# Fused attention, soft MoE and squared-ReLU FFN on one core: w_out slots 2 to 7 converted as pairs, the later m sums and the column sum as two fp32r products behind ReLU, two evictions ahead of a conversion

## The chip, the core and the metric

The kernel runs on one core of a Trainium2 chip. The metric is device time in microseconds (us) of the whole program. Three timed runs of the kernel before gave a median of 480.83 us (479.24 to 481.24). A fourth execution was recorded by the profiler.

## The reference

Three layers follow each other. All tensors are fp32.

```python
# 1. chunked attention: 4 batches, 8 heads, 768 positions, head size 64; chunks of 32 see 16 left, 8 right, 8 memory slots
a = softmax(q_c @ k_full.T / 8);  attn = a @ v_full          # -> x: (3072, 512)
# 2. soft MoE: 8 experts with 4 slots each
logits = x @ phi                                             # (3072, 32)
slot_input = softmax(logits, axis=0).T @ x                   # (32, 512)
slot_out = relu(slot_input[e] @ w1[e]) @ w2[e]               # (32, 512), F = 1024
y = softmax(logits, axis=1) @ slot_out                       # (3072, 512)
# 3. squared-ReLU FFN: d_ff = 2048
out = (s * relu(y @ w_in)**2 + b) @ w_out                    # (3072, 512)
```

## The kernel before

**Stages.** From the start to about 167 us the kernel runs attention, the routing softmaxes and the experts; the weights of the experts (w1, w2: 33.5 MB) stream from HBM through one queue on SP. From about 168 us to the end it runs the FFN, and there the change has its effect.

**The FFN's items.** y is never formed. Instead m = slot_out @ w_in (32 x 2048) is kept in `mpack`, and h = c @ m, with the routing weights c in `cpack`. The work is cut into 128 items, each one a block of 384 rows (b) with a slice of 128 of the 2048 hidden columns (f). Items 0 to 15 take blocks 0 and 1 in turn with f = 0 to 7, items 16 to 47 blocks 2 and 3 in turn with all 16 f, then come blocks 4 to 7 with 16 items each, and last the second halves of blocks 0 and 1. One item is

- on TensorE (PE): one product for h (`emit_h`, L825, 384 columns, fp32r), six products of 512 columns with the high half of w_out (`emit_o`, L877: three row tiles, once with the high and once with the low half of g) and three with its low half (`emit_o2`, L889);
- on ScalarE (ACT): ReLU (L831), square (L835), and the cast to the fp32r high half ghi (L839);
- on VectorE (DVE): the low half glo = g - ghi (`emit_g`, L842).

Iteration n of the main loop (it starts at n = 4) emits h of item n, ReLU, square and ghi of n, glo of n - 1, the high products of item n - 3 and the low products of n - 4. Each engine works through its instructions in the order in which the code emits them; a wait on one holds all behind it on that engine.

**Exact products.** TensorE's fp32r takes an operand rounded. So a factor is split in a rounded high half and the rest, and three products are added up. A plain fp32 product (L806, L812, L852) stands in the trace as two slower matmuls.

**Conversions.** w_in and w_out arrive as pairs of 16-bit halves. A slice of 512 columns is rebuilt by one ACT step (`cv_act`, L579) and by DVE steps: shift (L589), sign (L591), mask (L593), low part (L600). For w_out, ACT then casts the high half `whi` (L798) and DVE makes `wlo` in two steps (L791, L793). The table `cq` says at which iteration k which slice is converted: w_out slices f = 0 to 7 at k = 0, 2, ..., 14 (slice f is first used by item 2f), eight slices of w_in at k = 16 to 30, w_out slices 8 to 15 at k = 32 to 46. `stage_a`, `stage_d` and `stage_w` emit the steps of key k at iterations k - 1, k and k + 1. A w_out "slot" i holds the raw slices 2i and 2i + 1; three areas (NRG) take the raw slots in turn, and `load_w` at the loop's end loads the next one once the area's last use is over.

**The m sums.** `M_AT = (4, 26, 34)`: at these iterations `emit_m` forms a quarter of m in four row groups (L806), ACT copies it out of PSUM (`mps`, L808), one iteration later `emit_m2` adds the four groups up with a product by the 0/1 matrix `stks_all` (L812), and `m_split` writes `mpack` (ACT L817, DVE L818). The h products, the m sums and the column sum share two PSUM banks (tag "s"); a bank is taken again once the engines that read it are done. The sums are emitted ahead of the iteration's ReLU.

**Ends of blocks.** After the last f of a block the three accumulators are moved out of PSUM (L896 on DVE for tiles 0 and 2, L894 on ACT for tile 1) before the next block with the same banks may start. For blocks 0 and 1 this is at n = 18 and n = 19.

**Column sum.** At n = 64 `colsum` (L852) multiplies a matrix of ones with the sum of w_out to get b times the column sums, the `bias` of the later evictions.

## Time and profile before

| | |
|---|---|
| median of three runs | 480.83 us (479.24 to 481.24) |
| profiled execution | 479.52 us, of it 477.7 us from the first to the last instruction |
| PE busy | 456.7 us (96%) |
| DVE busy | 310.1 us (65%) |
| ACT busy | 308.7 us (65%) |
| granted TensorE clock | 1.00 of full speed |
| DMA | about 400 GB/s until 167 us, then under 170 GB/s |

Matmuls are pipelined: one is shown busy until its result has landed, and the next begins before that. So what a matmul costs is the time from its start to the next one's start, and a gap in a PE timeline is told by such starts.

### The profile page before, as it was taken

Reading aid. Unit: us, or ns where it says so; the run is one execution under the profiler, and the core shown is the slowest. Engines: PE = TensorE matmul, PEld = TensorE weight load, DVE = VectorE, ACT = ScalarE, POOL = GpSimd, SP = SyncE. Lnnn points to the kernel's source line nnn. Section 1 sums busy time; section 2 is a strip of 40 time slices with the busy share of each in tenths; the row PEclk is TensorE's granted clock in tenths of the full one; section 3 lists DMA queues with packets and bytes.
Section 4 is the critical chain, followed back from the end, with each engine's and each line's share of the span. In section 5 each row is a group of like instructions: output and inputs, shape, how many; then the busy total and the mean of one; then the engine's idle time right before and its main releaser. Section 6 shows DMA issues by size and latency. Waiting matters only on the chain.

```text
span 477.7 us, 10206 instructions
## 1 busy us (share of the span) xinstructions
PE 456.7 (96%) x3960; PEld 342.3 (72%) x3960; DVE 310.1 (65%) x685; ACT 308.7 (65%) x635; POOL 84.4 (18%) x154
## 2 busy tenths in 40 slices
PE   7899998999999999999898999999999999999996
PEld 5666666665555467868585888888888888888885
DVE  6778887885485889997484999975524224223232
ACT  4566666675144388888576897666666666666660
POOL 6666665650000000000000000007700000000000
PEclk9999999999999999999999999999999999999999
DMA  8999999999999934234222000003101001001011
GB/s 304 385 406 405 406 409 398 397 381 396 401 420 392 414 128 151 89 99 166 88 89 88 1 1 0 1 0 146 55 0 67 0 1 67 0 1 66 1 67 66
DMA packets 20576, 83.04 MB, mean 174 GB/s; under 512 B 2736, under 2 KB 2864, under 8 KB 14640
## 3 DMA queue, kind: packets, MB, share of 16 engines
q1 hardware_dynamic: 20528, 82.39, 44.6%
q8 instruction: 31, 0.51, 0.4%
q14 instruction: 17, 0.14, 0.1%
HBM read 76.09 MB, written 6.29 MB: 172 GB/s over the span
## 4 chain that ended last, share of the span: by engine, by line
PE 69%; DVE 13%; DMA 8%; ACT 4%; issue 3%; SPq 2%; POOL 1%; DVEq 0%; POOLq 0%; ACTq 0%
PE g L877 11%; PE lp L877 5%; PE pt L877 5%; PE x L877 5%; PE g L889 5%; PE xt L877 5%; PE s L825 4%; DMA seg<-in_w_dram 4%; PE s L630 3%; PE x L325 3%; DMA vals<-in_vm_dram 3%; PE lp L889 3%; PE pt L889 3%; PE xt L889 3%; PE x L889 3%
## 5 line engine op out<-in xcount | busy, mean ns | idle before, releaser
L842 DVE TENSOR_TENSOR glo<-r,ghi 128x384 fp32r<-128x384 f32 x128 | 76.3, 601 | 81.6 <-ACT ghi L839 81.4
L831 ACT ACTIVATE r<-s 128x384 f32<-128x384 f32 x128 | 62.8, 491 | 52.8 <-PE s L825 52.4
L835 ACT ACTIVATE r<-r 128x384 f32<-128x384 f32 x128 | 67.4, 527 | 6.2 <-DVE glo L842 2.0
L839 ACT CAST ghi<-r 128x384 fp32r<-128x384 f32 x128 | 65.7, 513 | 3.4
L825 PE MATMUL s<-cpack,mpack 128*128 128x384 f32 x128 | 44.2, 348 | 3.7 <-ACT r L831 2.1
L301 ACT ACTIVATE seg<-seg 128x384 f32<-128x384 f32 x32 | 28.8, 900 | 19.2 <-DVE seg L312 15.1
L889 PE MATMUL g<-wlo,ghi 128*128 128x512 f32 x128 | 40.2, 394 | 0.0
L877 PE MATMUL g<-whi,ghi 128*128 128x512 f32 x126 | 39.7, 394 | 0.2 <-DVE mpack L818 0.2
L877 PE MATMUL g<-whi,glo 128*128 128x512 f32 x126 | 39.3, 393 | 0.0
L864 POOL TENSOR_TENSOR keys<-keys,bias 128x512 f32<-128x512 f32 x6 | 8.4, 1426 | 168.7 <-DVE bias L853 168.7
L263 POOL TENSOR_SCALAR keys<-keys 64x416 f32<-64x416 f32 x63 | 33.7, 536 | 12.7 <-DMA keys<-in_kq_dram 7.5
L285 PE MATMUL s<-keys 128*32 128x128 f32 x768 | 30.3, 291 | 4.4 <-POOL keys L267 3.4
L825 PEld LDWEIGHTS s<-cpack,mpack 128*128 128x128 f32 x128 | 23.9, 188 | 13.0 <-ACT r L831 4.4
L325 PE MATMUL x<-vals,seg 128*32 128x128 f32 x744 | 28.0, 275 | 2.8 <-DMA vals<-in_vm_dram 2.0
L325 PEld LDWEIGHTS x<-vals,seg 128*32 128x32 f32 x744 | 20.3, 109 | 13.2 <-DVE seg L309 6.4
L889 PEld LDWEIGHTS g<-wlo,ghi 128*128 128x128 f32 x128 | 24.0, 188 | 5.3
L877 PEld LDWEIGHTS g<-whi,glo 128*128 128x128 f32 x126 | 23.7, 188 | 5.3
L285 PEld LDWEIGHTS s<-keys 128*32 128x32 f32 x768 | 19.5, 113 | 10.4 <-POOL keys L267 6.0
L319 ACT COPY seg<-pt 128x384 f32<-128x384 f32 x32 | 15.3, 478 | 17.9 <-PE pt L317 16.9
L877 PEld LDWEIGHTS g<-whi,ghi 128*128 128x128 f32 x126 | 23.7, 188 | 4.3 <-DVE mpack L818 0.7
L877 PE MATMUL lp<-whi,ghi 128*128 128x512 f32 x63 | 25.5, 404 | 0.9 <-DVE vals L896 0.9
L877 PE MATMUL pt<-whi,ghi 128*128 128x512 f32 x64 | 25.6, 400 | 0.0
(255 smaller groups left out, 991.1 us busy)
## 6 DMA issues: line engine op xcount, KB each, us to landing
seg<-in_w_dram SPq DMA_DIRECT2D x27, 1024.0 KB, 8.5
keys<-in_kq_dram SPq DMA_DIRECT2D x32, 396.0 KB, 7.4
vals<-in_vm_dram SPq DMA_DIRECT2D x64, 192.0 KB, 6.5
keys<-in_w_in_dram SPq DMA_DIRECT2D x5, 1024.0 KB, 5.1
keys<-in_w_out_dram SPq DMA_DIRECT2D x5, 1024.0 KB, 4.9
out_dram<-os SPq DMA_DIRECT2D x18, 256.0 KB, 2.1
vals<-in_w_in_dram SPq DMA_DIRECT2D x3, 1024.0 KB, 5.6
vals<-in_w_out_dram SPq DMA_DIRECT2D x3, 1024.0 KB, 4.9
```

The source lines that it names most:

```text
L263: (nc.vector if h and u == 0 else nc.gpsimd).tensor_scalar(out=stream(kz[rows, h], 0, CH), in0=k[rows, UT * h:UT * h + (NCU + 1) * CH].rea ...
L285: nc.tensor.matmul(out=o, lhsT=qt[:, 32 * c:32 * c + 32], rhs=kz[:, :, at:at + WIN], start=True, stop=not (first or last))
L301: nc.scalar.activation(out=p_r[u], in_=sm_r[u].rearrange("p t h (a r) -> p t r (h a)", a=2), func=AF.Exp, scale=scale)
L319: nc.scalar.copy(out=pts_r[u], in_=pt)
L325: nc.tensor.matmul(out=xp[32 * r:32 * r + 32, t], lhsT=pts_r[u][:, 32 * c:32 * c + 32], rhs=vbuf[u // 2 % 2][:, u % 2, :, 64 * c:64 * c + ...
L825: nc.tensor.matmul(out=hq, lhsT=mpack[:, 128 * f:128 * f + 128], rhs=cpack[:, b * UT:(b + 1) * UT], start=True, stop=True)
L831: nc.scalar.activation(out=r_g[n % 2], in_=h_t.pop(n), func=AF.Relu)
L835: nc.scalar.activation(out=r2_g[n % 2], in_=r_g[n % 2], func=AF.Square)
L839: nc.scalar.copy(out=ghi_g[n % (LA + 2)], in_=r2_g[n % 2])
L842: nc.vector.tensor_tensor(out=glo_g[n % (LA + 2)], in0=r2_g[n % 2], in1=ghi_g[n % (LA + 2)].bitcast(F32), op=ALU.subtract)
L877: nc.tensor.matmul(out=o_t[r_][t], lhsT=gt[:, 128 * t:128 * t + 128], rhs=w_hi[f], start=(f == r_[1] and gt is ghi), stop=False)
L889: nc.tensor.matmul(out=o, lhsT=ghi[:, 128 * t:128 * t + 128], rhs=w_lo[f], start=False, stop=(f == f1 - 1))
```

## The change

In the main loop:

- w_out slices 0 to 3 are converted as before. Slots 2 to 7 (slices 4 to 15) are converted as pairs of slices 1024 wide: `pair_a` (ACT) at iteration p0 - 1, shift and sign at p0, mask and low part and the cast `pair_hi` at p0 + 1, the two steps of `wlo` at p0 + 2 and p0 + 3, with p0 = 8, 11, 31, 34, 38 and 42 (table PS). All whi slices lie in one tile, all wlo slices in another. The conversion buffers and raw areas are placed elsewhere.
- `sums(n)` stands behind ReLU, square and ghi for n > 7. The second and third m sum and the column sum no longer use a plain fp32 product: `halves` makes a rounded copy on ACT (`mph`) and the rest on DVE (`mpl`), and `sum_of` multiplies both in fp32r.
- The conversion of iteration 18 is emitted in iteration 19, behind the evictions of block 1 (`convert(n - 1)`), and the load that would follow it waits for that, too.
- The load of the second raw slot is issued one step later in the w2 loop. Two small ACT instructions (`stkr`, `onesr`) make the fp32r matrices of the sums; a POOL memset of ones is gone.

```diff
--- before.py
+++ after.py
@@ -173,16 +173,16 @@
         at_.update({key: (18 + i) * SLOT for i, key in enumerate(EARLY)})
         cq = {}
         for j in range(8):
+            cq[16 + 2 * j] = ("i", 2 + j // 4, j % 4)
+        for j in range(4):
             cq[2 * j] = ("o", j)
-            cq[16 + 2 * j] = ("i", 2 + j // 4, j % 4)
-            cq[32 + 2 * j] = ("o", 8 + j)
-        raw_of = {("i", fb, j): ("wi", 2 * fb + j // 2) for fb in range(1, NFB) for j in range(4)}
-        raw_of.update({("o", f): ("wo", f // 2) for f in range(NF)})
-        last_use = {}
-        for k, key in sorted(cq.items()):
-            if raw_of[key] not in last_use:
-                order.append(raw_of[key])
-            last_use[raw_of[key]] = k
+
+        PS = {2: 8, 3: 11, 4: 31, 5: 34, 6: 38, 7: 42}
+        last_use = {("wi", 4 + j // 2): 16 + 2 * j for j in range(8)}
+        last_use.update({("wo", i): n + 1 for i, n in PS.items()})
+        last_use.update({("wo", 0): 2, ("wo", 1): 6})
+        order += [("wo", i) for i in range(4)] + [("wi", i) for i in range(4, 8)] + [("wo", i) for i in range(4, 8)]
+        RAW = [17 * SLOT, 18 * SLOT, 14 * SLOT]
         srcs = {"w1": w1, "w2": w2, "wi": w_in, "wo": w_out}
 
         wt = {}
@@ -193,7 +193,7 @@
                 i = wnext[0]
                 if i < (len(order) if cap is None else cap):
                     src = srcs[order[i][0]][order[i][1]]
-                    p = at_[order[i]] if i < npre else (16 + (i - npre) % NRG) * SLOT
+                    p = at_[order[i]] if i < npre else RAW[(i - npre) % NRG]
                     if p is SPLIT:
                         wt[order[i]] = [area(x, SLOT // 2) for x in p]
                         for x in range(2):
...
@@ -722,6 +722,10 @@
                 pk_p = ctx.enter_context(tc.tile_pool(name="pk", bufs=1, reuse_waits="tile"))
                 cpack = pk_p.tile([128, NT], F32R, name="cpack")
                 mpack = pk_p.tile([128, 128 * NF], F32R, name="mpack")
+                stkr = pk_p.tile([128, 128], F32R, name="stkr")
+                onesr = pk_p.tile([128, 128], F32R, name="onesr")
+                nc.scalar.copy(out=stkr, in_=stks_all)
+                nc.scalar.activation(out=onesr, in_=stks_all, func=AF.Copy, scale=0.0, bias=1.0)
             if i in (3, 7, 11):
                 emit_sos(i // 8, i // 4 % 2)
             if i in (4, 8, 12):
@@ -733,9 +737,7 @@
                 pack_c(i - 5)
             if i == 2:
                 load_w(len(EARLY) + E_AT)
-            if i == 10:
-                load_w(2)
-            if i == 14:
+            if i in (10, 11, 14):
                 load_w(1)
             if 11 <= i < 15:
                 warm(4)
@@ -751,13 +753,13 @@
         def tiles(name, n, w, dt=F32):
             return [g_p.tile([128, w], dt, name=f"{name}{i}") for i in range(n)]
 
-        w_hi, w_lo = tiles("whi", NF, DM, F32R), tiles("wlo", NF, DM, F32R)
-        os_g, mps = tiles("os", 3, DM), tiles("mps", 1, DM)[0]
+        wh_all, wl_all = (tiles(x, 1, NF * DM, F32R)[0] for x in ("whi", "wlo"))
+        w_hi, w_lo = ([t[:, DM * f:DM * f + DM] for f in range(NF)] for t in (wh_all, wl_all))
+        os_g, (mph, mpl) = tiles("os", 3, DM), tiles("mp", 2, DM, F32R)
         r_g, r2_g = (tiles(x, 2, UT) for x in ("r", "r2"))
         ghi_g, glo_g = tiles("ghi", LA + 2, UT, F32R), tiles("glo", LA + 2, UT, F32R)
-        wsum, bias = tiles("wsum", 1, DM)[0], tiles("bias", 1, DM)[0]
-        ones = tiles("ones", 1, 128)[0]
-        nc.gpsimd.memset(ones, 1.0)
+        wsum = tiles("wsum", 1, DM)[0]
+        bias = wsum
         HF = NF // 2
 
         runs = [[(0, 0, HF), (1, 0, HF)], [(2, 0, NF), (3, 0, NF)]]
@@ -770,13 +772,45 @@
         part = [tiles("part", 3, DM), [area(19 * SLOT + DM * t, DM) for t in range(NTU)]]
         h_t, o_t = {}, {}
 
+        cvs[:] = [area(15 * SLOT + 1536 * x, 3, 512) for x in range(2)]
+        pair = area(15 * SLOT, 3072).rearrange("p (x j f) -> p x j f", x=2, j=3)
+
+        def pair_w(i):
+            return wt["wo", i].rearrange("p (f d t) -> p f d t", f=2, t=2)
+
+        def pair_a(i):
+            nc.scalar.activation(out=pair[:, :, 0, :], in_=pair_w(i)[:, :, :, 1].bitcast(F32), func=AF.Copy,
+                                 scale=2.0 ** -112)
+
+        def pair_hi(i):
+            nc.scalar.copy(out=two(wh_all, i), in_=pair[:, :, 2, :])
+
+        def two(t, i):
+            return t[:, 2 * DM * i:2 * DM * (i + 1)].rearrange("p (x f) -> p x f", x=2)
+
+        def pair_d(i, step):
+            h, lf, a = (pair[:, :, j, :] for j in range(3))
+            hi, ai, w = h.bitcast(I32), a.bitcast(I32), pair_w(i)
+            if step == 0:
+                nc.vector.tensor_scalar(out=hi, in0=hi, scalar1=3, scalar2=None, op0=ALU.logical_shift_left)
+                nc.vector.scalar_tensor_tensor(out=ai, in0=w[:, :, :, 1], scalar=SIGN, in1=hi, op0=ALU.bitwise_and,
+                                               op1=ALU.bitwise_or)
+            elif step == 1:
+                nc.vector.tensor_scalar(out=hi, in0=ai, scalar1=EXPM, scalar2=None, op0=ALU.bitwise_and)
+                nc.vector.scalar_tensor_tensor(out=lf, in0=w[:, :, :, 0].bitcast(U32), scalar=2.0 ** -52, in1=h,
+                                               op0=ALU.mult, op1=ALU.mult)
+            elif step == 2:
+                nc.vector.tensor_tensor(out=a, in0=a, in1=two(wh_all, i).bitcast(F32), op=ALU.subtract)
+            else:
+                nc.vector.tensor_tensor(out=two(wl_all, i), in0=a, in1=lf, op=ALU.add)
+
         def stage_a(k):
             key = cq.get(k)
             if key:
                 if key[0] == "i":
                     w = wi_src(key[1], key[2])
                 else:
-                    w = wt[raw_of[key]].rearrange("p (f d t) -> p f d t", f=2, t=2)[:, key[1] % 2]
+                    w = wt["wo", key[1] // 2].rearrange("p (f d t) -> p f d t", f=2, t=2)[:, key[1] % 2]
                 cv_act(key, k // 2 % 2, w)
 
         def stage_d(k, j):
@@ -805,11 +839,25 @@
                     lhsT, rhs = (soTb[:, kc, :], wis_l[:, kc, :]) if lo else (soT4[:, kc, 0, :], wis[kc // 2][:, kc % 2, :])
                     nc.tensor.matmul(out=mp[32 * kc:32 * kc + 32, :], lhsT=lhsT, rhs=rhs,
                                      start=(lo == 0), stop=(lo == 1 or fb == 1))
-            nc.scalar.copy(out=mps, in_=mp)
+            if fb == 1:
+                nc.scalar.copy(out=os_g[0], in_=mp)
+            else:
+                halves(mp)
+
+        def halves(x):
+            nc.scalar.copy(out=mph, in_=x)
+            nc.vector.tensor_tensor(out=mpl, in0=x, in1=mph.bitcast(F32), op=ALU.subtract)
+
+        def sum_of(out, lhsT):
+            for x in (mph, mpl):
+                nc.tensor.matmul(out=out, lhsT=lhsT, rhs=x, start=(x is mph), stop=(x is mpl))
 
         def emit_m2(fb):
             mr = psum("s", [128, 512])
-            nc.tensor.matmul(out=mr, lhsT=stks_all, rhs=mps, start=True, stop=True)
+            if fb == 1:
+                nc.tensor.matmul(out=mr, lhsT=stks_all, rhs=os_g[0], start=True, stop=True)
+            else:
+                sum_of(mr, stkr)
             m_split(mr, 512 * fb, slice(0, 512))
 
         def m_split(mp, base, cols):
@@ -849,7 +897,8 @@
 
         def colsum():
             c = psum("s", [128, DM])
-            nc.tensor.matmul(out=c, lhsT=ones, rhs=wsum, start=True, stop=True)
+            halves(wsum)
+            sum_of(c, onesr)
             nc.vector.tensor_scalar(out=bias, in0=c, scalar1=sbt[:, 1:2], scalar2=None, op0=ALU.mult)
 
         def store(b, t, os_):
@@ -914,6 +963,19 @@
         def stages(n, *js):
             for j in js:
                 stage_d(n, j)
+
+        def sums(n):
+            if n in M_AT:
+                emit_m(M_AT.index(n) + 1)
+            if n - 1 in M_AT:
+                emit_m2(M_AT.index(n - 1) + 1)
+
+        def convert(n):
+            stage_d(n, 1)
+            stage_w(n)
+            stages(n, 2, 3)
+            stages(n - 1, 4, 5)
+            stage_d(n + 1, 0)
 
 
         cp = (nc.scalar.copy, nc.vector.tensor_copy)
@@ -973,6 +1035,8 @@
             late = m + 1 < len(items) and m + 1 == 2 * HF + 1
             if ends or late:
                 emit_o2(m)
+            if n == 2 * HF + 3:
+                convert(n - 1)
             if 1 < m + 1 < len(items):
                 emit_o(m + 1)
             if m > 1 and not ends and not late:
@@ -981,21 +1045,26 @@
                 emit_h(n)
             if n == 6:
                 nc.vector.tensor_copy(out=soTb, in_=soT4[:, :, 0, :])
-            if n in M_AT:
-                emit_m(M_AT.index(n) + 1)
-            if n - 1 in M_AT:
-                emit_m2(M_AT.index(n - 1) + 1)
+            if n <= 7:
+                sums(n)
             emit_relu(n)
             emit_sq(n)
             stage_a(n + 1)
             emit_ghi(n)
+            if n > 7:
+                sums(n)
             if LA + 1 < n <= len(items):
                 emit_g(n - 1)
-            stage_d(n, 1)
-            stage_w(n)
-            stages(n, 2, 3)
-            stages(n - 1, 4, 5)
-            stage_d(n + 1, 0)
+
+            if n != 2 * HF + 2:
+                convert(n)
+            for i, p0 in PS.items():
+                if n == p0 + 1:
+                    pair_hi(i)
+                if 0 <= n - p0 < 4:
+                    pair_d(i, n - p0)
+                if n == p0 - 1:
+                    pair_a(i)
             if 48 <= n < 64:
                 for i in (2 * n - 96, 2 * n - 95):
                     wsum_add(i)
@@ -1003,7 +1072,7 @@
                 colsum()
             if 65 <= n < 77:
                 add_bias(n - 65)
-            while wnext[0] < len(order) and last_use.get(order[wnext[0] - NRG], -1) <= n:
+            while n != 2 * HF + 2 and wnext[0] < len(order) and last_use.get(order[wnext[0] - NRG], -1) <= n:
                 load_w(1)
```

The order of instructions at three places. On ACT around the second m sum (iterations 26 and 27; `r` with `s` is ReLU, `mps` or `mp0` the copy of the sum, `mpack` the result), before:

```order
L831 ACTIVATE r1_2659<-s_3175 128x384
L835 ACTIVATE r21_2661<-r1_2659 128x384
L579 ACTIVATE keys_102<-keys_102 128x512
L839 CAST ghi0_2662<-r21_2661 128x384
L808 COPY mps0_2657<-s_3203 128x512
L831 ACTIVATE r0_2658<-s_3192 128x384
L835 ACTIVATE r20_2660<-r0_2658 128x384
L839 CAST ghi1_2663<-r20_2660 128x384
L817 CAST mpack_2427<-s_3232 128x512
L831 ACTIVATE r1_2659<-s_3221 128x384
```

and after:

```order
L879 ACTIVATE r0_2633<-s_3148 128x384
L883 ACTIVATE r20_2635<-r0_2633 128x384
L887 CAST ghi1_2638<-r20_2635 128x384
L848 CAST mp0_2631<-s_3162 128x512
L879 ACTIVATE r1_2634<-s_3178 128x384
L883 ACTIVATE r21_2636<-r1_2634 128x384
L579 ACTIVATE keys_102<-vals0_103 128x512
L887 CAST ghi2_2639<-r21_2636 128x384
L865 CAST mpack_2427<-s_3193 128x512
L879 ACTIVATE r0_2633<-s_3200 128x384
```

The copy of the sum moved behind ReLU, square and ghi of iteration 26, and the copy to mpack behind those of iteration 27.

On DVE around the ends of blocks 0 and 1 (`part` and `vals` are the evicted accumulators, L589 to L600 the conversion), before:

```order
L589 TENSOR_SCALAR keys_102<-keys_102 128x512
L896 TENSOR_SCALAR part0_2676<-pt_2724,cstt_65 128x512
L896 TENSOR_SCALAR part2_2678<-xt_2726,cstt_65 128x512
L842 TENSOR_TENSOR glo2_2669<-r21_2661,ghi2_2664 128x384
L591 SCALAR_TENSOR_TENSOR seg26624_99<-keys_102 128x2x256
L593 TENSOR_SCALAR keys_102<-seg26624_99 128x512
L600 SCALAR_TENSOR_TENSOR seg48784_101<-keys_102 128x2x256
L896 TENSOR_SCALAR vals1_104<-lp_2741,cstt_65 128x512
L896 TENSOR_SCALAR vals1_104<-g_2743,cstt_65 128x512
```

and after:

```order
L589 TENSOR_SCALAR keys_102<-keys_102 128x512
L945 TENSOR_SCALAR part0_2648<-pt_2696,cstt_65 128x512
L945 TENSOR_SCALAR part2_2650<-xt_2698,cstt_65 128x512
L890 TENSOR_TENSOR glo2_2644<-r21_2636,ghi2_2639 128x384
L945 TENSOR_SCALAR vals1_104<-lp_2713,cstt_65 128x512
L945 TENSOR_SCALAR vals1_104<-g_2715,cstt_65 128x512
L591 SCALAR_TENSOR_TENSOR seg26624_99<-vals0_103,keys_102 128x2x256
L593 TENSOR_SCALAR keys_102<-seg26624_99 128x512
L600 SCALAR_TENSOR_TENSOR seg48784_101<-vals0_103,keys_102 128x2x256
```

Three conversion steps moved behind the two evictions of block 1.

On DVE in iterations 8 to 11 (the conversion of slices 4 and 5), before, where slice 4 takes the first seven rows and slice 5 begins in the eighth:

```order
L589 TENSOR_SCALAR seg26624_99<-seg26624_99 128x512
L842 TENSOR_TENSOR glo2_2669<-r21_2661,ghi2_2664 128x384
L591 SCALAR_TENSOR_TENSOR seg26624_99<-vals0_103,seg26624_99 128x512
L593 TENSOR_SCALAR seg26624_99<-seg26624_99 128x512
L600 SCALAR_TENSOR_TENSOR seg26624_99<-vals0_103,seg26624_99 128x512
L842 TENSOR_TENSOR glo3_2670<-r20_2660,ghi3_2665 128x384
L791 TENSOR_TENSOR seg26624_99<-seg26624_99,whi4_2626 128x512
L793 TENSOR_TENSOR wlo4_2642<-seg26624_99 128x512
L589 TENSOR_SCALAR keys_102<-keys_102 128x512
```

and after:

```order
L890 TENSOR_TENSOR glo2_2644<-r21_2636,ghi2_2639 128x384
L795 TENSOR_SCALAR keys_102<-keys_102 128x2x512
L796 SCALAR_TENSOR_TENSOR keys_102<-seg26624_99,keys_102 128x2x512
L890 TENSOR_TENSOR glo3_2645<-r20_2635,ghi3_2640 128x384
L799 TENSOR_SCALAR keys_102<-keys_102 128x2x512
L800 SCALAR_TENSOR_TENSOR keys_102<-seg26624_99,keys_102 128x2x512
L890 TENSOR_TENSOR glo4_2646<-r21_2636,ghi4_2641 128x384
L803 TENSOR_TENSOR keys_102<-keys_102,whi0_2626 128x2x512
L890 TENSOR_TENSOR glo0_2642<-r20_2635,ghi0_2637 128x384
L805 TENSOR_TENSOR wlo0_2627<-keys_102 128x1024
```

The wlo of slice 4 (L793 before, L805 after) moved from behind the second glo to behind the fourth, and each step is twice as wide.

## Rows read from the trace of the kernel before

**Rows 1.** Busy time by stretch: stretch, length, PE, PEld, DVE, ACT, POOL, clock, DMA

```profile
187.00:207.00 20.00, 20.00 (x91) 16.52 (x90) 19.55 (x38) 18.15 (x38) 0.00 (x0) 1.00 0.39 129
260.00:320.00 60.00, 60.00 (x268) 49.54 (x267) 56.00 (x99) 47.20 (x94) 0.00 (x0) 1.00 0.00 1
```

**Rows 2.** Timeline of PE, one undisturbed item: start, duration, engine, line, operation

```profile
316.85 0.34 PE L825 MATMUL s<-cpack,mpack 128*128 128x384 f32 x1
317.03 0.40 PE L877 MATMUL pt<-whi,ghi 128*128 128x512 f32 x1
...
319.11 0.34 PE L825 MATMUL s<-cpack,mpack 128*128 128x384 f32 x1
```

**Rows 3.** Timeline of PE, items 26 to 29, around the second m sum

```profile
226.85 0.34 PE L825 MATMUL s<-cpack,mpack 128*128 128x384 f32 x1
...
230.08 0.40 PE L806 MATMUL s<-seg 128*32 128x512 bf16 x4
231.16 0.45 PE L825 MATMUL s<-cpack,mpack 128*128 128x384 f32 x1 [0.68 <-ACT mps L808]
...
233.50 1.02 PE L812 MATMUL s<-mps,stk 128*128 128x512 f32 x2
235.59 0.44 PE L825 MATMUL s<-cpack,mpack 128*128 128x384 f32 x1 [1.07 <-ACT r L831]
...
237.94 0.34 PE L825 MATMUL s<-cpack,mpack 128*128 128x384 f32 x1
```

**Rows 4.** Waits, 225 to 262 us: who for whom, us in total, times, longest

```profile
DVE mpack L818 <- ACT mpack L817: 9.8, 2, 5.8
...
PEld s L825 <- ACT r L831: 3.8, 2, 1.9
```

**Rows 5.** Timeline of ACT in the same stretch

```profile
230.52 0.59 ACT L808 COPY mps<-s 128x512 f32<-128x512 f32 x1 [3.54 <-PE s L806]
...
234.56 0.59 ACT L817 CAST mpack<-s 128x512 fp32r<-128x512 f32 x1 [1.96 <-PE s L812]
235.04 0.50 ACT L831 ACTIVATE r<-s 128x384 f32<-128x384 f32 x1
```

**Rows 6.** Timeline of PE, items 18 to 21, the ends of blocks 0 and 1

```profile
206.98 0.34 PE L825 MATMUL s<-cpack,mpack 128*128 128x384 f32 x1
...
213.87 0.50 PE L877 MATMUL lp<-whi,ghi 128*128 128x512 f32 x1 [0.85 <-DVE vals L896]
...
215.56 0.34 PE L825 MATMUL s<-cpack,mpack 128*128 128x384 f32 x1
```

**Rows 7.** Timeline of DVE in the same stretch

```profile
211.28 0.69 DVE L591 SCALAR_TENSOR_TENSOR seg<-keys 128x512 int32<-128x512 int32 x1
...
213.07 0.75 DVE L896 TENSOR_SCALAR vals<-lp,cstt 128x512 f32<-128x512 f32 x1
```

**Rows 8.** Timelines of PE (items 64 to 66) and of ACT around the column sum

```profile
321.37 0.34 PE L825 MATMUL s<-cpack,mpack 128*128 128x384 f32 x1
...
323.63 1.02 PE L852 MATMUL s<-wsum,ones 128*128 128x512 f32 x2
...
326.73 0.34 PE L825 MATMUL s<-cpack,mpack 128*128 128x384 f32 x1
...
322.83 0.51 ACT L839 CAST ghi<-r 128x384 fp32r<-128x384 f32 x1
```

**Rows 9.** Timelines of DVE, ACT and PE where slice 4 is converted

```profile
188.40 0.42 DVE L589 TENSOR_SCALAR seg<-seg 128x512 int32<-128x512 int32 x1
188.74 0.55 DVE L842 TENSOR_TENSOR glo<-r,ghi 128x384 fp32r<-128x384 f32 x1
189.21 0.68 DVE L591 SCALAR_TENSOR_TENSOR seg<-vals,seg 128x512 int32<-128x512 int32 x1
...
185.53 0.62 ACT L798 CAST whi<-keys 128x512 fp32r<-128x512 f32 x1 [0.81 <-DVE keys L591]
...
191.20 0.34 PE L825 MATMUL s<-cpack,mpack 128*128 128x384 f32 x1
```

More of the change, by code (lines that the diff above doesn't have):

```diff
@@ L565 @@
         cvs = [area((14 + i) * SLOT, 3, 512) for i in range(2)]
-        soT4 = area(15 * SLOT + 1536, KD, 4, NS)
-        sos_r = Ring(14 * SLOT + 1536, 2, 256)
+        soT4 = area(16 * SLOT + 1024, KD, 4, NS)
+        sos_r = Ring(16 * SLOT + 1536, 2, 256)
         ck_r = [area(p, 4, 4, NS).bitcast(F32R) for p in range(11 * SLOT, 11 * SLOT + NT, 512)]
```

## The prediction, made before the changed kernel ran

> **What bounds the kernel now.** I read the busy time by stretch first, then the PE timeline by the starts of h, then who waits for whom at each place where these starts are too far apart. In the FFN PE is the bound nearly everywhere: from 260 to 320 us it is busy all of 60.00 us [rows 1]. An undisturbed item takes 319.11 - 316.85 = 2.26 us, of which h takes 0.18 and each of the nine 512-wide products (319.11 - 317.03) / 9 = 0.231 us [rows 2]. 128 items at this pace are 289 us; the change doesn't touch that. It touches what lies above it, at three places. (1) The second and the third m sum: items 26 to 29 take 237.94 - 226.85 = 11.09 us where three items take 6.78, so one sum costs 4.31 us [rows 3]; the wait behind it occurs twice in 225 to 262 us, once for each sum [rows 4]. (2) The ends of blocks 0 and 1: items 18 to 21 take 215.56 - 206.98 = 8.58 us, 1.80 too many [rows 6]. (3) The column sum: items 64 to 66 take 5.36 us, 0.84 over two items [rows 8]. Before 168 us the stream of weights sets the time (the DMA line of the table above), and the change there is two small ACT steps and one load.
>
> **Base.** The sum is made against the profiled execution, 479.52 us (span 477.7). It lies 1.3 us under the median of the three timed runs, which spread over 2.0 us; one execution can't say which of the four is typical, so I put the result against the mean of all four, 480.2.
>
> **The m sums.** What of the 4.31 us is work? The ten products of item 26 end their turn at 226.85 + 2.26 = 229.11. The last of the four-group products starts at 230.08 and holds PE 0.23 us, to 230.31: 1.20 us of work that stays. The fp32 product of L812 holds PE from 233.50; a 512-wide fp32r product takes 0.23, and at the column sum the same fp32 form pushed the following work back by 0.84 us [rows 8], so I count 0.86. Work is 1.20 + 0.86 = 2.06, and 2.25 us are waits. The trace names them: h of item 27 starts at 231.16, behind the ACT copy of the sum (it takes over that PSUM bank), and h of item 28 at 235.59, behind a ReLU that began at 235.04 because the copy to mpack, which waited for the sum's second product, stood ahead of it on ACT [rows 3, 5]. After, ReLU 26 and 27 run ahead of these copies, so h 27 takes the bank that ReLU 26 frees, long done, and h 28 the bank of the sum, free once `mph` and `mpl` are made. The added step is one DVE subtraction between copy and product: copy 0.59 [rows 5], subtraction at most 0.75 (the widest 512-wide DVE row, [rows 7]), about 1.4 us with the hand-overs, while PE has an item of 2.26 us to do before it needs them. So it is hidden with 0.9 us to spare. Left of a sum: 1.20 + 2 x 0.231 and some 0.1 for weight loads after a change of form = 1.75 us. Bounds: 1.66 (no such 0.1) and 2.3 (half a wait of 0.6 left). Gain 4.31 - 1.75 = 2.56 each, **5.1 us** for two. Queued behind the subtraction on DVE is glo of the item before; it is needed two items later, 4.5 us, so no stall.
>
> One new wait follows the second of them. The bank of its result is free for h of item 37 only when DVE has done the mpack subtraction, and that stands behind the last step of pair 4 and the first two of pair 5, each about twice as long as a 512-wide step. From the end of the four-group products: copy and subtraction to 1.35, glo 0.5, one step 1.2, shift and sign 1.9, subtraction 0.6: 5.5 us; h 37 is due at 0.18 + 2.08 + 0.46 + 0.1 + 2.26 = 5.1. Cost 0.4 to 0.9, taken **+0.6**. The first sum has narrow steps there and is free a microsecond before it is needed.
>
> **The ends.** The end of block 1 costs most: PE waits until 213.87 for an eviction [rows 6] that DVE begins only at 213.07, after three conversion steps from 211.28 on [rows 7]. These take 213.07 - 211.28 = 1.79 us and now stand behind. What is late next: the accumulators of block 1 are complete about 1 us into item 19, two evictions of 0.75 end 1.5 us later, and PE needs the first bank one item after that. At n = 15 to 17 DVE has only narrow steps of one slice, so it isn't behind by then. I take 1.80 to 0.1, **-1.7** (bounds -1.3, since a part of it falls to block 0, whose evictions DVE also began late, and -1.8). The three steps themselves go into item 19 and 20, whose DVE has room for them; the load held back there is needed nine items later.
>
> **The column sum.** This is a loss. Before, the product waits for nothing and costs 0.84. After, `mph` stands behind ghi of item 64 on ACT, which starts at 322.83 and lasts 0.51 [rows 8]: copy about 323.3 to 323.9, subtraction to 324.65, second product 324.7 to 324.95. Before, h 65 could follow at 323.63 + 0.86 = 324.49. So **+0.45** (bounds 0.2, if ACT is early, and 0.8).
>
> **The pairs.** Two sizes: DVE and ACT time, and when a slice is ready. Time: 128 columns more cost 0.68 - 0.55 = 0.13 us on DVE [rows 9], so 512 more cost 0.5 to 0.55, and a two-source step of 1024 about 1.2 us. The shift at 0.42 is quicker than that slope allows and is bounded by 0.42 (free) and 0.84 (double); I take 0.7. A pair is then 4 x 1.2 + 2 x 0.7 = 6.2 us; two slices are 2 x (4 x 0.68 + 2 x 0.42) = 7.1. With four glo of 0.5 that makes 8.2 us and 9.1 in four items, which are 9.04 us of PE. On ACT 0.62 - 0.51 = 0.11 per 128 columns makes the 1024-wide cast 1.05 us. Readiness: now slice 4 has its wlo behind the second glo, after the change behind the fourth. In 187 to 207 us DVE is busy 19.55 of 20.00 us [rows 1], so it runs behind PE there and the delay isn't hidden. I follow the queue from the rows. DVE comes to glo 7 at about 188.40 (the shift of slice 4, which began there, is gone) [rows 9]: glo to 188.87, shift and sign to 190.8. The cast to whi needs this on ACT, 190.85 to 191.9. Item 8's high products are due in iteration 11, at 191.20 + 0.18 = 191.4 [rows 9]: 0.5 us late. Then glo 0.5, mask and low 1.85, glo 0.5, subtraction 1.15, glo 0.5, last step 1.2: wlo at 196.4. The low products of item 8 come 2.26 + 0.18 + 1.39 after 191.20, plus the 0.5 just lost: 195.5. 0.9 us late. From pair 3 on, the same queue leaves the products at or just after their data, since pair 3 is first needed at item 12 and PE has been put back. **+1.3**; bounds 0 (DVE catches up elsewhere) and 2.5 (pair 3 late by as much). Pairs 4 to 7 have items 31 to 45 for slices first used at items 32 to 47 of blocks 2 and 3, each one 1 to 2 us ahead by the same count: 0, beside the 0.6 above.
>
> The rows show DVE nearly full for 20 us [rows 1] and PE at full pace. The Trainium skill, page "Perfetto Trace Analysis", section "Optimizing Scalar/DVE Operations", says that grouping into larger operations can improve throughput if the engine is saturated, but that an engine which isn't saturated yet causes bubbles elsewhere may do better with instructions broken up. By its first half the pairs are free and the sum is that of the first rival; by its second the 1.3 us stand.
>
> **Nothing from:** the start (the load of the second raw slot is issued later, but still while expert weights that were issued earlier fill the one queue, and nothing stands behind it on SP that is needed earlier; the two ACT steps lie where ACT waits for PE anyway), the POOL memset, the tail.
>
> **Sum.** -5.1 + 0.6 - 1.7 + 0.45 + 1.3 = -4.45 us: 475.1 for the profiled execution, **475.7** against the mean.
>
> **Rivals.** (a) The pairs cost nothing: DVE saves about a microsecond a pair and catches up. For it: pairs need 8.2 of 9.04 us where single slices need 9.1. Against: the first pair is late at once. 475.7 - 1.3 = 474.4. (b) The new waits come out at their bounds: h finds its bank held by the DVE subtraction in both sums, 0.9 us each (+1.2), and the pairs cost 2.5 (+1.2). For it: both hang on one queue that is full [rows 1]. Against: the first sum has a microsecond of room. 475.7 + 2.4 = 478.1. (c) The change doesn't do what it says: PE waits for `mpl` instead of for ReLU, because DVE is late when the copy is done. It decides if DVE is more than 0.9 us behind then; before, DVE waits there twice, 9.8 us in all [rows 4], so hardly. All 5.1 us return: 480.8, no change. (d) Slower: the pairs starve PE throughout. Place: the DVE queue in items 8 to 15 and 31 to 46. It decides if a pair with its glo takes over 9.04 us, that is if 1024-wide steps cost more than twice the narrow ones or ACT's waits for DVE add up; then each of six pairs costs what the first does, 1.3, and the second sum's 0.6 doubles: 475.7 + 5 x 1.3 + 0.6 = 482.8.
>
> **How the numbers follow.** Chances: forecast 0.60, (a) 0.22, (b) 0.10, (c) 0.05, (d) 0.03. The forecast's own bounds, with the runs' spread of a microsecond, are 474.3 to 477.3; taking in (a) and most of (b) the range is 473.4 to 478.2. About 0.5% (2.4 us) is what a measurement of this kernel can tell from no change: under 477.8 lie the forecast, (a) and some of (b), faster 0.86; the rest of (b) and (c), same 0.11; slower 0.03.
>
> **What would show it.** In the trace after: items 26 to 29 and 34 to 37 in 8.5 and 9.1 us; no wait of PE for an eviction at the ends; 1.2 us over two items at 64; and a wait of PE for whi or wlo at item 11 or 12. Wrong I'd be if the h starts of items 8 to 16 or 31 to 47 are spread by much more, or if the FFN starts later than 168 us.

## The result, and the profile after

| | before | after |
|---|---|---|
| median | 480.39 us (479.24 to 481.32, 6 runs) | 475.89 us (475.56 to 476.68, 6 runs) |
| profiled execution, its span | 479.52, 477.7 us | 476.45, 474.7 us |
| h of item 0, h of item 127, the time between | 167.87, 464.59, 296.71 us | 168.86, 461.53, 292.67 us |

The ratio is 0.9909 [0.9891, 0.9927], that is -4.5 us: 0.9% faster, with an interval clear of 1, and 0.2 us from the predicted 475.7. In the two traces the FFN, from the first h to the last, is shorter by 4.04 us. The first h lies 1.0 us later after; over the ten profiles of this study it lies between 167.87 and 170.55 us, so one profile of each can't say whether the change put it there. I compare the time between first and last h, and give it for every run.

What follows goes through the places where the starts of h are further apart than the 2.26 us of an undisturbed item. The excess of a place is the sum of what each of its items takes above 2.26 us, from the start of its h to the start of the next; an item that is a few hundredths short isn't set off, so an excess can lie up to 0.06 us above what the first and the last start give. It is good to 0.01 or 0.02 us. In the page's own view of the engines little is seen: PE is busy 455.1 us (456.7 before) and DVE 307.7 (310.1 before).

**The second m sum.** PE's timeline after (start, duration, engine, line, operation), to be laid beside [rows 3]:

```profile
227.59 0.34 PE L873 MATMUL s<-cpack,mpack 128*128 128x384 f32 x1
...
230.82 0.40 PE L840 MATMUL s<-seg 128*32 128x512 bf16 x4
231.15 0.44 PE L873 MATMUL s<-cpack,mpack 128*128 128x384 f32 x1
231.43 0.40 PE L926 MATMUL pt<-whi,ghi 128*128 128x512 f32 x1
...
233.48 0.64 PE L853 MATMUL s<-mp,stkr 128*128 128x512 f32 x2
233.95 0.34 PE L873 MATMUL s<-cpack,mpack 128*128 128x384 f32 x1
236.19 0.34 PE L873 MATMUL s<-cpack,mpack 128*128 128x384 f32 x1
```

No h has a bracket with a wait any more. Three items take 236.19 - 227.59 = 8.60 us, 1.82 more than three undisturbed ones (before 4.31). Counted item by item the excess is 1.85, and that figure is used from here on. And the ACT and DVE steps between, to be laid beside [rows 5]:

```profile
231.26 0.59 ACT L848 CAST mp<-s 128x512 fp32r<-128x512 f32 x1 [1.70 <-PE s L840]
231.74 0.50 ACT L879 ACTIVATE r<-s 128x384 f32<-128x384 f32 x1
...
231.88 0.69 DVE L849 TENSOR_TENSOR mp<-s,mp 128x512 fp32r<-128x512 f32 x1 [4.11 <-ACT mp L848]
```

The subtraction ends at 232.57; PE asks for it with the second of the two products, at about 233.48 + 0.23 = 233.71. ReLU stands at 231.74 and is no longer held.

**The third m sum** costs the same 1.85 us, and then 0.69 more: PE and DVE after.

```profile
253.85 0.34 PE L873 MATMUL s<-cpack,mpack 128*128 128x384 f32 x1
...
256.71 0.44 PE L873 MATMUL s<-cpack,mpack 128*128 128x384 f32 x1 [0.47 <-DVE mpack L866]
...
252.85 1.22 DVE L805 TENSOR_TENSOR wlo<-keys 128x1024 fp32r<-128x1024 f32 x1
253.98 0.69 DVE L795 TENSOR_SCALAR keys<-keys 128x1024 int32<-128x1024 int32 x1
254.71 1.23 DVE L796 SCALAR_TENSOR_TENSOR keys<-keys 128x1024 int32<-128x1024 int32 x1
255.96 0.69 DVE L866 TENSOR_TENSOR mpack<-s,mpack 64x512 fp32r<-64x512 f32 x1
```

Three steps of pairs stand ahead of the mpack subtraction, and h of item 37 waits for the bank that this one reads.

**The first pair.** From item 9 to item 13 it is 1.59 us more than four undisturbed items (before 0.04, by the starts of these two). PE, then ACT and DVE, to be laid beside [rows 9]:

```profile
190.13 0.44 PE L873 MATMUL s<-cpack,mpack 128*128 128x384 f32 x1
...
192.47 0.34 PE L873 MATMUL s<-cpack,mpack 128*128 128x384 f32 x1
193.68 0.49 PE L926 MATMUL pt<-whi,ghi 128*128 128x512 f32 x1 [0.88 <-ACT whi L786]
...
188.56 1.14 ACT L782 ACTIVATE keys<-seg 128x1024 f32<-128x1024 f32 x1
189.61 0.47 ACT L879 ACTIVATE r<-s 128x384 f32<-128x384 f32 x1
...
192.16 0.52 ACT L887 CAST ghi<-r 128x384 fp32r<-128x384 f32 x1
192.59 1.04 ACT L786 CAST whi<-keys 128x1024 fp32r<-128x1024 f32 x1
...
190.59 1.23 DVE L796 SCALAR_TENSOR_TENSOR keys<-seg,keys 128x1024 int32<-128x1024 int32 x1
...
196.14 1.22 DVE L805 TENSOR_TENSOR wlo<-keys 128x1024 fp32r<-128x1024 f32 x1
```

DVE's sign step is done at 191.82, but the cast begins at 192.59 only, right behind ghi: on ACT it stands behind the ReLU, square and ghi of an item, and ACT works from 187.06 us to there without a gap. In the table of waits of 186 to 198 us (who for whom: total, times, longest) the wait for wlo is a small one:

```profile
PEld pt L938 <- DVE wlo L805: 0.3, 1, 0.3
```

A part of the excess stands ahead of both. The ReLU of item 8 begins at 189.61, behind the 1.14 us of `pair_a`, and ends at 190.08; h of item 10 takes over the bank that it reads, and starts at 190.13. Items 9 and 10 take 192.47 - 187.60 = 4.87 us, 0.27 more than before (191.20 - 186.60 = 4.60).

**The ends.** Item 19 starts at 209.51, item 20 at 211.77, item 21 at 214.03: every 2.26 us, no wait [rows 6]. The evictions on DVE wait for PE now, and the conversion stands behind them [rows 7]:

```profile
212.38 0.75 DVE L945 TENSOR_SCALAR vals<-lp,cstt 128x512 f32<-128x512 f32 x1 [0.39 <-PE lp L938]
...
213.70 0.68 DVE L591 SCALAR_TENSOR_TENSOR seg<-vals,keys 128x512 int32<-128x512 int32 x1
```

**The column sum** [rows 8]. PE and ACT after; its two products don't stand together, since the second waits for the subtraction:

```profile
317.82 0.34 PE L873 MATMUL s<-cpack,mpack 128*128 128x384 f32 x1
...
320.36 0.49 PE L853 MATMUL s<-mp,onesr 128*128 128x512 f32 x1
321.09 0.51 PE L853 MATMUL s<-mp,onesr 128*128 128x512 f32 x1 [0.23 <-DVE mp L849]
321.43 0.33 PE L873 MATMUL s<-cpack,mpack 128*128 128x384 f32 x1
...
319.69 0.61 ACT L848 CAST mp<-wsum 128x512 fp32r<-128x512 f32 x1
```

321.43 - 317.82 = 3.61 us for one item, an excess of 1.35 (before 0.83 over two items).

### The profile page after: what moved, and what is told of

It reads as the page before. It is cut to its first block, busy times and chain, and to the rows that moved or that the text cites. A ratio compares the mean times of both kernels' runs of the same rounds, so it can differ in the third digit from the quotient of the medians.

```text
span 474.7 us, 10173 instructions
## 1 busy us (share of the span) xinstructions
PE 455.1 (96%) x3960; PEld 342.3 (72%) x3960; DVE 307.7 (65%) x652; ACT 308.4 (65%) x626; POOL 83.9 (18%) x153
## 4 chain that ended last, share of the span: by engine, by line
PE 67%; DVE 12%; DMA 8%; ACT 7%; issue 2%; SPq 2%; POOL 1%; DVEq 0%; POOLq 0%; ACTq 0%
PE g L926 10%; PE g L938 5%; PE pt L926 5%; PE lp L926 5%; PE x L926 5%; PE xt L926 5%; DMA seg<-in_w_dram 5%; PE s L873 4%; PE s L630 3%; PE x L325 3%; PE lp L938 3%; PE pt L938 3%; PE xt L938 3%; PE x L938 3%; PE s L285 2%
## 5 line engine op out<-in xcount | busy, mean ns | idle before, releaser
L913 POOL TENSOR_TENSOR keys<-keys,wsum 128x512 f32<-128x512 f32 x6 | 8.4, 1428 | 195.1 <-ACT r L879 195.1
L938 PE MATMUL pt<-wlo,ghi 128*128 128x512 f32 x64 | 25.5, 398 | 0.2 <-DVE wlo L827 0.2
```

Of the source, the lines that this page charges most:

```text
L938: nc.tensor.matmul(out=o, lhsT=ghi[:, 128 * t:128 * t + 128], rhs=w_lo[f], start=False, stop=(f == f1 - 1))
```

## The experiments

Excess in us at each place, from the starts of h in one profile of each kernel. The second and third sum are items 26 to 29 and 34 to 38 (39 where waits go on), the ends items 19 to 21, the column sum 64 to 66. The first pair is items 9 to 12; for `pair2_early` item 8 is taken in, less the 0.17 that it takes above 2.26 us in the kernel before. From h of item 0 to h of item 8 all ten kernels take the same, 16.29 to 16.32 us. A ratio is to the runs of the kernel before in the same batch, whose medians are 480.39, 480.44 and 480.34.

| kernel | first pair | ends | second sum | third sum | column sum | h 0 to h 127 | median, ratio to before |
|---|---|---|---|---|---|---|---|
| before | 0.08 | 1.81 | 4.32 | 4.34 | 0.83 | 296.71 | |
| after | 1.59 | 0 | 1.85 | 2.54 | 1.35 | 292.67 | 475.89, 0.9909 [0.9891, 0.9927] |
| order_only | 0.08 | 1.80 | 2.24 | 2.24 | 0.83 | 292.50 | 476.49, 0.992 [0.9892, 0.9948] |
| products_only | 0.07 | 1.77 | 4.32 | 4.32 | 0.83 | 296.69 | 480.17, one run (before 480.34) |
| sums_only | 0.09 | 1.78 | 1.85 | 3.01 | 0.83 | 292.86 | 476.7, 0.9914 [0.9885, 0.9943] |
| evict_only | 0.09 | 0.46 | 4.32 | 4.32 | 0.83 | 295.36 | 479.18, 0.997 [0.9947, 0.9994] |
| no_pairs | 0.11 | 0.51 | 1.85 | 3.02 | 1.34 | 292.08 | 475.3, 0.9883 [0.983, 0.9936] |
| pair2_early | 1.78 | 0 | 1.85 | 2.54 | 1.35 | 292.87 | 478.33, one run (before 480.34) |
| late_pairs | 0.08 | 0.51 | 1.85 | 2.54 | 1.35 | 291.61 | 475.49, 0.9896 [0.9876, 0.9916] |
| best | 0.05 | 0.47 | 1.85 | 1.85 | 0.47 | 289.98 | 473.68, 0.9873 [0.9851, 0.9895] |

The medians move as the FFN does, to about half a microsecond, but for `pair2_early`, whose FFN starts at 170.55 in the one execution there is. They also bear on the start of the FFN: median less FFN is 183.2 to 183.9 us in `after`, `no_pairs`, `late_pairs` and `best`, which issue the loads as the change does, and 183.5 to 184.0 in the five that issue them as before. So no later start shows in the medians.

**Is it the order or the products that make the sums cheaper?** `order_only` is the kernel before with the sums behind ReLU, square and ghi, and nothing else (fp32 product, narrow slices):

```diff
-            if n in M_AT:
-                emit_m(M_AT.index(n) + 1)
-            if n - 1 in M_AT:
-                emit_m2(M_AT.index(n - 1) + 1)
+            if n <= 7:
+                sums(n)
             emit_relu(n)
             emit_sq(n)
             stage_a(n + 1)
             emit_ghi(n)
+            if n > 7:
+                sums(n)
```

> The kernel before with the m sums behind ReLU, square and ghi, but the product still plain fp32. Theory (the waits go by the order alone; the form of the product is worth 0.4 us a sum): a sum costs 1.2 + 0.86 + 0.1 = 2.2 us in place of 4.31, -4.2 us, about 476.2, and no wait for DVE, since there is no subtraction ahead of the product. Rival (the products carry half of the gain or more): -2 us or less.

`products_only` leaves the sums ahead of ReLU and replaces the product; `sums_only` does both.

```diff
-            nc.scalar.copy(out=mps, in_=mp)
+            if fb == 1:
+                nc.scalar.copy(out=os_g[0], in_=mp)
+            else:
+                halves(mp)
...
-            nc.tensor.matmul(out=mr, lhsT=stks_all, rhs=mps, start=True, stop=True)
+            if fb == 1:
+                nc.tensor.matmul(out=mr, lhsT=stks_all, rhs=os_g[0], start=True, stop=True)
+            else:
+                sum_of(mr, stkr)
```

> The kernel before with the second and third m sum as two fp32r products, but still ahead of ReLU. Theory (the wait comes from the order on ACT): PE saves 0.4 us a sum, and waits as much longer, since ReLU still stands behind the copies and a subtraction is added: a sum costs 4.2 to 4.6 us, no gain. Rival (the products carry part of the gain by themselves): 3.9 us or less a sum.

> The kernel before with one part of the change: the second and third m sum behind ReLU, square and ghi, and as two fp32r products. Slices stay 512 wide, the column sum is plain fp32, the evictions stay where they were. Theory (waits behind the sums' copies on ACT, and one wait for a bank that comes from the 1024-wide steps): each sum falls from 4.31 to about 1.85 us as in the changed kernel, and with narrow steps there is no wait of h 37 for its bank: -4.9 us, about 475.5. Rival A (the bank wait comes from a full DVE queue, wide steps or not): the second sum keeps 1 us or more of its wait: -3.5 to -4, about 476.7. Rival B (the sums gain only together with the pairs): under -2 us.

The order alone takes 4.32 to 2.24 at each sum, the products alone take nothing. PE of `products_only`, where h waits for ReLU at both copies as before:

```profile
232.20 0.44 PE L842 MATMUL s<-cpack,mpack 128*128 128x384 f32 x1 [1.07 <-ACT r L848]
...
236.24 0.44 PE L842 MATMUL s<-cpack,mpack 128*128 128x384 f32 x1 [1.07 <-ACT r L848]
```

PE of `order_only`, where no h waits and the fp32 product holds PE for about 0.85 us (h of the next item starts at 233.66 but its products at 234.24, 0.58 later, where 0.18 is usual):

```profile
233.21 1.02 PE L812 MATMUL s<-mps,stk 128*128 128x512 f32 x2
233.66 0.74 PE L825 MATMUL s<-cpack,mpack 128*128 128x384 f32 x1
234.24 0.39 PE L877 MATMUL lp<-whi,ghi 128*128 128x512 f32 x1
```

With both, the second sum is at 1.85: the products are worth 2.24 - 1.85 = 0.39 a sum, and only once the waits are gone. But the third sum is at 3.01 in `sums_only`, 0.77 over `order_only`, and there are no pairs in this kernel: its expectation, no wait there with narrow steps, failed. PE, ACT and DVE show what waits:

```profile
254.10 0.45 PE L842 MATMUL s<-cpack,mpack 128*128 128x384 f32 x1 [0.62 <-ACT r L848]
...
250.63 0.59 ACT L817 CAST mp<-s 128x512 fp32r<-128x512 f32 x1 [1.71 <-PE s L809]
253.04 0.62 ACT L801 CAST whi<-keys 128x512 fp32r<-128x512 f32 x1 [1.83 <-DVE keys L591]
253.56 0.48 ACT L848 ACTIVATE r<-s 128x384 f32<-128x384 f32 x1
...
251.25 0.69 DVE L818 TENSOR_TENSOR mp<-s,mp 128x512 fp32r<-128x512 f32 x1 [4.10 <-ACT mp L817]
...
252.32 0.69 DVE L591 SCALAR_TENSOR_TENSOR keys<-vals,keys 128x512 int32<-128x512 int32 x1
```

The narrow slice's cast stands on ACT between the sum's copy and the next ReLU. It waits 1.83 us for DVE's sign step, which the new subtraction has put back: that one stands on DVE for 4.10 us until the sum's copy is done, with the sign step behind it. ReLU and h wait behind the cast. It isn't the bank that the mpack subtraction holds. At the second sum the slices converted are of w_in, which have no such cast.

**The eviction's order.** `evict_only` is the kernel before with the conversion of iteration 18 emitted behind the evictions of block 1, and the load held back with it.

```diff
+            if n == 2 * HF + 3:
+                convert(n - 1)
...
+            if n != 2 * HF + 2:
+                convert(n)
```

> The kernel before with one part of the change: the conversion of iteration 18 behind the evictions of block 1. Theory (PE waits for an eviction that stands behind three conversion steps of 1.8 us): items 18 to 21 take 6.9 to 7.3 us in place of 8.58, -1.3 to -1.7 us, about 478.9. Rival (DVE is behind anyway without the pairs, so the evictions are late all the same): over 8 us, under -0.6.

The ends go from 1.81 to 0.46, not to 0. What is left stands in block 0's eviction, at item 19: 212.46 - 209.74 = 2.72 us, in PE's timeline.

```profile
209.74 0.34 PE L825 MATMUL s<-cpack,mpack 128*128 128x384 f32 x1
...
212.46 0.34 PE L825 MATMUL s<-cpack,mpack 128*128 128x384 f32 x1
```

DVE comes to that eviction late: it begins it without a wait of its own, and the first product into the bank starts at 210.77.

```profile
209.97 0.75 DVE L896 TENSOR_SCALAR part<-pt,cstt 128x512 f32<-128x512 f32 x1
```

**The pairs.** `no_pairs` is the kernel after with all slices narrow and at their old iterations. `late_pairs` has narrow slices in slots 2 and 3, and pairs in 4 to 7. `pair2_early` begins pair 2 an iteration earlier.

```diff
-        for j in range(4):
+        for j in range(8):
             cq[2 * j] = ("o", j)
-
-        PS = {2: 8, 3: 11, 4: 31, 5: 34, 6: 38, 7: 42}
+            cq[32 + 2 * j] = ("o", 8 + j)
+
+        PS = {}
...
```

> The changed kernel with slices 4 to 15 converted one by one, 512 wide, at the old iterations; all else as changed. Theory (pairs only cost: 1.5 us at items 9 to 12 and 0.7 at item 36): items 9 to 13 at 2.26 us each, -2.2 us against the changed kernel, about 473.7. Rival (the DVE time that pairs save is needed at the third sum and at the ends): the 1.5 us come back in part, through a longer wait in items 35 to 38 or an eviction that is late: 474.5 to 476.

```diff
-        for j in range(4):
+        for j in range(8):
             cq[2 * j] = ("o", j)
 
-        PS = {2: 8, 3: 11, 4: 31, 5: 34, 6: 38, 7: 42}
+        PS = {4: 31, 5: 34, 6: 38, 7: 42}
...
```

> The changed kernel with slices 4 to 7 one by one as before, and pairs only for slices 8 to 15. Theory (pairs cost 1.5 us at items 9 to 12, save 0.5 at the end of block 0 and 0.5 in items 35 to 39): the waits at 9 to 12 are gone, 0.5 at item 19 is back, the third sum stays at 2.5 us: the main loop's span from the first to the last h is 1.0 us shorter than in the changed kernel, 291.7 us, and 0.4 shorter than without any pair. Rival (early pairs are needed for the ends): over 1 us comes back at items 19 and 20, no gain.

```diff
-        PS = {2: 8, 3: 11, 4: 31, 5: 34, 6: 38, 7: 42}
+        PS = {2: 7, 3: 11, 4: 31, 5: 34, 6: 38, 7: 42}
```

> The changed kernel with the pair of slices 4 and 5 begun one iteration earlier (p0 = 7 in place of 8). Theory as it now stands (VectorE's queue is full there, so that two slices at once make others late, whenever they start): the 1.5 us of waits at items 9 to 12 stay, 1.2 to 1.8, but move to items 8 and 9, where glo or wlo of the narrow slices comes late. Rival (the pair is only begun too late for its first user): the waits fall to 0.3 or less.

Without pairs the stall from item 9 on is gone (1.59 to 0.11), but 0.51 comes back at the ends and 3.02 - 2.54 = 0.48 at the third sum. So all pairs together cost 292.67 - 292.08 = 0.59 us, as the rival in the expectation had it. What the ends give back is read from DVE, which has next to no idle time from 187 us up to there. The last glo ahead of block 0's evictions, and the shift behind it, which waits for ACT, in DVE's timeline after:

```profile
207.75 0.55 DVE L890 TENSOR_TENSOR glo<-r,ghi 128x384 fp32r<-128x384 f32 x1
209.25 0.43 DVE L589 TENSOR_SCALAR keys<-keys 128x512 int32<-128x512 int32 x1 [0.95 <-ACT keys L579]
```

the same glo, and the eviction, in that of `no_pairs`:

```profile
209.77 0.55 DVE L890 TENSOR_TENSOR glo<-r,ghi 128x384 fp32r<-128x384 f32 x1
...
210.69 0.75 DVE L945 TENSOR_SCALAR part<-pt,cstt 128x512 f32<-128x512 f32 x1
```

Counted from the first h, that glo starts at 38.89 us after and at 40.71 in `no_pairs`: DVE gets there 1.82 us earlier with two pairs, and then waits. At most 0.3 of that is less idle time (19.79 and 19.51 us busy in 187 to 207 us, rows below), the rest is less work. In `no_pairs` it comes to the evictions late, without a wait.

With pairs 4 to 7 alone the kernel has the gain at the third sum and not the stall: 291.61. The medians of the three lie within 0.6 us and can't rank them; the traces can. Beginning pair 2 earlier doesn't remove the stall, it moves it to item 8. PE and ACT of `pair2_early`:

```profile
190.96 0.44 PE L873 MATMUL s<-cpack,mpack 128*128 128x384 f32 x1 [1.50 <-ACT r L879]
...
189.40 1.14 ACT L782 ACTIVATE keys<-seg 128x1024 f32<-128x1024 f32 x1 [0.56 <-DVE keys L600]
```

`pair_a` waits until DVE has left slice 3, whose buffer it shares, and ReLU, which begins at 190.43, stands behind its wait and its 1.14 us. The expectation had the place and the size right, but not the cause: it looked for a late glo or wlo.

**A kernel from these readings.** `best` is `late_pairs` with pairs 5 to 7 two iterations later, so that none of their steps stands ahead of the mpack subtraction, and with the column sum's halves ahead of ReLU 64. Its edit against `late_pairs`:

```diff
-        PS = {4: 31, 5: 34, 6: 38, 7: 42}
+        PS = {4: 31, 5: 36, 6: 40, 7: 44}
...
             c = psum("s", [128, DM])
-            halves(wsum)
             sum_of(c, onesr)
...
+            if n == 64:
+                halves(wsum)
             emit_relu(n)
```

> The changed kernel with slices 4 to 7 one by one, pairs 5, 6 and 7 begun two iterations later (36, 40, 44), and the halves of the column sum made ahead of ReLU of iteration 64. Theory (h 37 waits for a bank that the mpack subtraction frees, behind the steps of pair 5; the column sum waits for a copy behind ghi): no wait at item 36 (0.7 us less), the column sum at 0.5 us in place of 1.35 (0.85 less), 1.0 less from the early slices: main loop 290.1 us, 2.5 under the changed kernel, about 473.4 in all. Rival (VectorE is full and gives the 0.7 back at items 38 to 47): 290.8 to 291.5.

The wait at item 36 is gone, and the column sum costs its two products. PE of `best`, third sum and column sum:

```profile
251.92 0.34 PE L873 MATMUL s<-cpack,mpack 128*128 128x384 f32 x1
254.16 0.34 PE L873 MATMUL s<-cpack,mpack 128*128 128x384 f32 x1
...
317.44 0.64 PE L853 MATMUL s<-mp,onesr 128*128 128x512 f32 x2
317.91 0.34 PE L873 MATMUL s<-cpack,mpack 128*128 128x384 f32 x1
```

473.68 us, 6.7 under the kernel before (480.34 in that batch) and, by the FFN, 2.69 under the kernel after.

## Why the prediction was right, and where its steps were not

The time, the sign and the size came out: -4.45 us forecast, -4.50 measured. The terms, against the traces:

- **The m sums**, -5.1 forecast, (1.85 - 4.32) + (1.85 - 4.34) = -4.96 measured. Right, and the cause with it: the order took away the two waits (`order_only` -2.08 a sum, `products_only` 0). A sum is 0.1 us dearer than forecast, and nothing waits in it. The term that was cut too fine is the 0.1 for the change of form. It came out at 0.2: h of item 27 starts 0.33 us behind the last of the four-group products (231.15 - 230.82), where 0.23 was counted, and its own products 0.28 behind it (231.43 - 231.15), where 0.18 is usual. That weight loads are the reason, as the prediction has it, is shown by no run.
- **The bank wait of h 37**, +0.6 forecast, +0.69 measured, at that item and for that reason in the kernel after. The attribution of it to the width of the steps fails as an account of what the pairs do: `sums_only` and `no_pairs`, with narrow steps, lose 3.01 - 1.85 = 1.16 there. They lose it otherwise, by a cast on ACT that waits for DVE. The prediction looked only at what stands ahead of the mpack subtraction, not at what the new subtraction of `halves` pushes back on DVE and who on ACT waits for that.
- **The ends**, -1.7 forecast, -1.81 measured: the sum right, its cause right in part. Moving the conversion is worth 1.35 (`evict_only`); the other 0.46 leaves only in the kernels with pairs 2 and 3. The prediction credited all to the move because it took DVE not to be behind at iterations 15 to 17; with narrow slices in slots 2 and 3 it is, and the 1.82 us that DVE is earlier with the pairs, more than the 0.46 needed, would end that. The prediction had that saving (7.1 - 6.2 = 0.9 us a pair) and gave it no use. PE's own delay of 1.5 us in these kernels gives DVE time, too. Either is larger than the 0.46; what each would do alone wasn't tried.
- **The column sum**, +0.45 forecast, +0.52 measured, by the step that was named: `mph` behind ghi of item 64.
- **The pairs**, +1.3 forecast, +1.55 measured at items 9 to 12, in other parts. The queue of DVE was followed rightly: sign step done at 190.8 on the clock of before, which with the FFN's 1.0 us later start is 191.8 (191.82 measured), and wlo at 196.4, so 197.4 (196.14 + 1.22 = 197.36 measured). But whi was expected at once behind the sign step, and it came 0.77 us later, because ACT works in order and had ReLU, square and ghi ahead of the cast. So whi was about a microsecond late instead of 0.5, PE was put back by that, and wlo cost 0.1 (the start of the next h) to 0.3 (the wait row) instead of 0.9. The two come to 1.55 - 0.27 = 1.28, next to the 1.3 forecast, though neither had its forecast size: that is luck. The other 0.27, h of item 10 behind a ReLU behind `pair_a`, the prediction didn't have: it followed DVE's queue and left out what the 1024-wide steps put back on ACT.
- **What the pairs cost in all** was put at these 1.3, and 1.9 with the bank wait that was laid to their width, and is 0.59: the step that failed is the 0 for what they give back, 0.46 to 0.51 at the ends and 0.48 at the third sum.

Together: -4.96 + 0.69 - 1.81 + 0.52 + 1.55 = -4.01 us, where the FFN moved by -4.04 and the medians by -4.50. The half microsecond between is within the runs' spread. What was laid to the wrong part of the change at the ends and at the third sum stood in the sum with the right size. So the total didn't show it, which is luck as far as the mechanism goes; only the kernels with one part undone did.

Of the rivals, pairs that cost nothing (474.4) and pairs that starve PE throughout (482.8) both fall, the first by the stall at items 9 to 12, the second by the absence of such a stall at 31 to 47, where only the bank wait of h 37 is seen. The first was right in that DVE's saving is real (1.82 us by the ends); it didn't make up for the stall. New waits at their bounds (478.1) fall with the second sum, which has none. PE waiting for `mpl` (480.8) is seen in one place, the column sum, with 0.23 us. As to the rule on larger operations (the Trainium skill, page "Perfetto Trace Analysis", section "Optimizing Scalar/DVE Operations"), both halves show at the early pairs. Grouping did let DVE through its work sooner (1.82 us at the ends), and yet caused bubbles on PE, although DVE was all but full: in 187 to 207 us DVE is busy 19.79 us after and 19.51 in `no_pairs`, and PE 19.10 and 20.00. Busy time by stretch, columns as in [rows 1], after:

```profile
187.00:207.00 20.00, 19.10 (x83) 14.89 (x82) 19.79 (x28) 19.09 (x36) 0.00 (x0) 1.00 0.47 159
```

and in `no_pairs`:

```profile
187.00:207.00 20.00, 20.00 (x90) 16.39 (x89) 19.51 (x37) 18.14 (x38) 0.00 (x0) 1.00 0.33 111
```

So with DVE 98 to 99% busy, what the first product that needs the pair waited for weighed more (1.55 us) than the throughput gained: without the early pairs `late_pairs` is 292.67 - 291.61 = 1.06 us shorter.

Open: whether the change moves the start of the FFN by less than the spread of the runs; the medians show no move.

## What to carry to other kernels

On an engine that works in order, a copy that feeds a rare step cost nothing here by itself; what cost was what stood behind it while it waited. So put it behind the work that the next item needs, and then make its own work smaller: the second gained nothing here without the first. Where a step is added, list who waits for the steps that it pushes back on its engine, on other engines too. A sum that comes out isn't evidence for its terms: undo one part at a time, since here two terms were credited, in whole or in part, to the wrong part of the change.

## What the runs show of the hardware

A 512-wide plain fp32 product costs PE about 0.85 us here (in `order_only` 0.45 to the start of h and 0.58 - 0.18 in h) and two fp32r products of the same width 0.47 (317.91 - 317.44), which agrees with the 0.39 a sum; 0.86 was forecast from the column sum. On DVE 1024-wide steps with two tensor inputs take 1.22 us (512 wide 0.69), and the one-source shift 0.69 (512 wide 0.42), close to what was estimated from narrower rows (1.2 and 0.7): either way one wide step is about 0.15 us shorter than two narrow ones. On ACT the 1024-wide cast takes 1.04 us (512 wide 0.62): in one piece, it holds everything behind it on that engine 1.7 times as long as a narrow one. The cost of that is what wasn't expected.
